# One Gelu for all MLP rows on ScalarE, with a changed start and end, in a fused attention and token-MLP kernel

## The chip, the cores and the metric

One core of a Trainium2 chip runs the kernel. The metric is the device time in microseconds of one execution. Before the change it is 704.06 us, the median of 3 runs (704.04 to 705.08).

## What is computed

The input x has 2048 rows of 512 columns. Two branches read its layer norm, and both are added to x.

```python
x = A_x
xn = _layernorm(x, axis=-1)
return x + _A_ref(xn, A_wqkv, A_wo) + _B_ref(xn, B_w1, B_b1, B_w2, B_b2)
# _A_ref: full softmax attention, H = 32 heads of Dh = 16 over S = 2048 rows
qkv = split(x @ wqkv);  scores = einsum("bhqd,bhkd->bhqk", q, k) * Dh ** -0.5
o = einsum("bhqk,bhkd->bhqd", softmax(scores), v);  return o @ wo
# _B_ref: an MLP over the rows (tokens), F = 1376
h = _layernorm(x);  u = gelu(einsum("bsd,sf->bdf", h, w1) + b1)   # tanh form of gelu
y = einsum("bdf,fs->bds", u, w2) + b2;  return y.transpose(0, 2, 1)
```

Inputs and output are bf16.

## The kernel before

**Attention.** Queries are cut into 4 query blocks of 512, heads into 8 groups of four. A pair of these is a block: 32 blocks in all (NBLK), and each has 16 key tiles of 128 keys. One key tile of one block is a score group, 512 of them (NGRP): four score products (line 558, K = 16 padded to 32 rows, four side by side in the array), each 128 keys by 512 queries. Its exponentials are taken in one of two ways:

- On ScalarE: two ACTIVATE Exp of 128 x 1024, each over two PSUM banks (line 566, tile pT). One PV pass of four products follows (line 578).
- On VectorE: four first passes that add a bias to the scores and write them as int16, which read as bf16 is an approximate power of two (line 612), and then two more planes shifted by a constant (line 617; NPL = 3 planes). Three PV passes follow. The planes lie in buffers of 128 x 2048 that are named after the memory they borrow: plx, which is their own, and x_sb, xn_sb, h_sb, w1blk and others once those are done with.

The PV result of a block lies in bank 6 and is copied by VectorE (line 1073). The denominators are inverted and spread out by small DMAs on SP's queue and POOL multiplies (line 1110, tiles oT and otmp).

**The dispatcher.** The order of every engine's instructions is fixed when the kernel is built. A dispatcher plays the program forward with its own planned costs (`occ`, `lat`) and at each step gives an engine the next thing that is ready. TensorE's rules are in `pe_step` and `pe_fill`: refill ScalarE's two bank pairs (banks 0 to 3) with scores as soon as they are free, give VectorE scores in banks 4, 5 and 7 when it has room, and otherwise issue PV passes and products of the side work. `d_pick1` decides which group VectorE may take: in the current block as long as D_KEEP groups remain open, at most D_AHEAD of the next, and in the last block only if it would be done before ScalarE (constant D_LAST). Side work is a list of chains (K, V and Q projections, the MLP), each with a due time in units of blocks. `two=True` marks VectorE instructions that the dispatcher keeps apart from long POOL instructions; planes are among them, first passes are not.

**The MLP.** After the second layer norm there are eleven chains `chain_ut`, one for each tile of 128 of the 1376 hidden rows (the last has 96): 16 products into one bank, a VectorE copy to u_sb with half of the bias (line 869), two VectorE products (lines 873 and 876), a ScalarE Tanh (line 879), and a VectorE product into gT (line 884). When all eleven are done (`ut_done`), sixteen chains `chain_yo` multiply gT with w2, one for each 128 output rows, in the order of `yt_order`. For the first three query blocks they add the attention's output product and x and store. For the last query block they put MLP + x into `part` (line 972), and the tail adds the attention.

**Start.** x comes in eight DMAs on SP's queue (four single tiles first), the first K and Q weights on ScalarE's queue. LN statistics of four tiles (NPRE), transposes, and the first K and Q tiles are written out by hand before the dispatcher starts.

**End.** Three output products and half of a fourth are done for each of the last four row tiles in banks 0 to 3 once ScalarE has no group left. `tail_epilogue` then takes the last block through VectorE in two halves of 256 columns (transpose, reciprocal, product, transpose: lines 1695 to 1703), ends the product (line 913), adds `part` on VectorE four times (line 1711) and stores on SP's queue.

Of the kernel before, what the change touches and what calls it, by code (L numbers as in the profile page):

```python
# [257 lines left out]
def bass_parallel_sum__softmax_full_mha__mixer_token_mlp__prompt_kernel(  # L258
# [18 lines left out]
    with ExitStack() as es:  # L277
# [32 lines left out]
        plx = sb("plx", [128, 2048], BF16)  # L310
# [10 lines left out]
        u_sb = sb("u_sb", [128, 512], F32)  # L321
        ga_sb = sb("ga_sb", [128, 512], F32)
# [36 lines left out]
        NPRE = 4  # L359

# [12 lines left out]
        def v_consts(i, eng):  # L373
# [5 lines left out]
            if i == 0:  # L379
                sc.add("dve", lambda e: e.memset(main[:, :, 16:17], 1.0), writes=[("Vone",)], occ=620)  # L380
# [12 lines left out]
        def ld_x(a, b_, lat):  # L393
            dma("sp", x_sb[:, a:b_, :],
                x2[128 * a:128 * b_, :].rearrange("(t p) d -> p t d", p=128),
                reads=[], writes=[("x", t) for t in range(a, b_)], name="ld_x", lat=lat)

        def ld_w(j, T0_, T1_, lat, q="act"):
# [4 lines left out]

        sc.add("act", lambda e: e.activation(r2[:, 0:1], zw[:, 0:1], ACTF.Identity), reads=[("zw",)], writes=[("r2",)],
               occ=1700)
# [22 lines left out]
        def late_consts():  # L428
# [10 lines left out]
            sc.add("dve", lambda e: e.tensor_scalar(b1h[:], b1c_bf[:], 0.5, None, ALU.mult), reads=[("b1c",), ("b1c2",)],  # L439
# [158 lines left out]
        plane_add(plx[:, :], [], "own")  # L598
# [99 lines left out]
        k_mm(1, 3, 0)  # L698
        qt0_mm(2, QB)
        ln_stats(NPRE)  # L700
        qt0_mm(3, 4)
        qt_evac(0, QB, "act", 0, 384)
        qt_evac(0, 4, "act", 384, 512, "QTh")
        k_mm(2, 3, 1)
        k_mm(3, 3, 2)
        qt_evac(1, 4, "act", 384, 512, "QTh")
        qt_evac(1, QB, "act", 0, 384)
        k_evac(1, 3, 3, 0)
# [25 lines left out]
        ut_done = [0]  # L734
        yo_done = {qb: 0 for qb in range(NQB)}
# [115 lines left out]
        def chain_ut(ft, due, rel):  # L851
# [15 lines left out]
            def u_evac():  # L867
                xb = bk[0]
                return sc.add("dve", lambda e: e.tensor_scalar(
                    u_sb[0:m, :], bank(xb)[0:m, :], 0.5, b1h[0:m, ft:ft + 1], ALU.mult, ALU.add),  # L870
                    reads=[("bank", xb), ("b1h",)], writes=[("u",)], occ=650, lat=800)
            steps.append(Step("dve", u_evac, 650, gate=lambda: ut_done[0] == ft, frees=True))
            steps.append(Step("dve", lambda: sc.add("dve", lambda e: e.scalar_tensor_tensor(
                ga_sb[0:m, :], u_sb[0:m, :], 4.0 * GELU_A, u_sb[0:m, :], ALU.mult, ALU.mult),
                reads=[("u",)], writes=[("ga",)], two=True, **T_DVE(512)), 610, two=True))
            steps.append(Step("dve", lambda: sc.add("dve", lambda e: e.scalar_tensor_tensor(
                ga_sb[0:m, :], ga_sb[0:m, :], 1.0, u_sb[0:m, :], ALU.add, ALU.mult),
                reads=[("ga",), ("u",)], writes=[("ga",)], two=True, **T_DVE(512)), 610, two=True))
            steps.append(Step("act", lambda: sc.add("act", lambda e: e.activation(  # L879
                ga_sb[0:m, :], ga_sb[0:m, :], ACTF.Tanh, scale=2.0 * GELU_C),  # L880
                reads=[("ga",)], writes=[("ga",)], occ=500, lat=680), 500))

            def fin():
                op = sc.add("dve", lambda e: e.scalar_tensor_tensor(
# [361 lines left out]
        def d_pick1():  # L1246
            skip()
            if ga[0] >= NGRP:
                return None
# [555 lines left out]
```

## Time and profile before

| | |
|---|---|
| median of 3 runs | 704.06 us (704.04 to 705.08) |
| the profiled execution | 704.31 us, its span 702.5 us |
| granted TensorE clock | 1.000 |
| exponentials on ScalarE (line 566) | 734 |
| first exponential starts | 11.45 us |
| MLP hidden tiles, copies of line 869 | 144.9 to 313.4 us |
| HBM read, written | 26.08 MB, 2.61 MB |

A busy share is the time in which an engine had at least one instruction in it. Instructions of one engine overlap at their ends, so a mean duration is longer than the distance between two starts. Matmul ends are modelled. "Idle before" names what ended the wait. Rows of a timeline begin with the start and the time taken in us.

### The profile page before, as it was taken

To read this page: it belongs to the slowest core of one execution; us is meant where nothing else is said; L and a number is where in the kernel's file an instruction comes from. 1 tells how busy PE (TensorE), PEld (TensorE's weight loads), DVE (VectorE), ACT (ScalarE), POOL (GpSimd) and SP (SyncE) were. 2 spreads that over 40 slices of the span, in tenths; PEclk is the share of its full clock that TensorE was granted. 3 is DMA by queue.
4 is the path that set the end of the run, shared out by engine and by line. 5 is a ranking of instruction groups with operands and counts; after the bars stand their busy time and mean duration, and the time that the engine had idled before them with its cause. 6 is when DMAs were issued, how large, how long until landed. Compare 5 with 4: busy or idle time off the path is not lost.

```text
span 702.5 us, 15631 instructions
## 1 busy us (share of the span) xinstructions
PE 670.9 (95%) x6238; PEld 200.8 (29%) x6238; DVE 665.5 (95%) x1155; ACT 684.5 (97%) x754; POOL 61.0 (9%) x89
## 2 busy tenths in 40 slices
PE   8999999999999999999999999999999999999987
PEld 4533333222222222222222222222222222222222
DVE  7889999999999999999999999999999999999998
ACT  6999999999999999999999999999999999999994
POOL 4510100000000000000000000000000000000000
PEclk9999999999999999999999999999999999999999
DMA  7024110022312132002221212111221022101001
GB/s 210 1 61 88 36 26 18 13 50 54 74 32 50 43 72 46 17 14 61 60 55 50 61 41 51 53 43 46 50 52 36 23 52 53 27 28 34 2 29 46
DMA packets 78368, 32.66 MB, mean 46 GB/s; under 512 B 63004, under 2 KB 74204, under 8 KB 78296
## 3 DMA queue, kind: packets, MB, share of 16 engines
q1 hardware_dynamic: 77240, 31.40, 18.2%
q8 instruction: 49, 0.80, 0.5%
q10 hardware_dynamic: 1056, 0.26, 0.2%
q14 instruction: 23, 0.19, 0.1%
HBM read 26.08 MB, written 2.61 MB: 41 GB/s over the span
## 4 chain that ended last, share of the span: by engine, by line
ACT 82%; PE 12%; DVE 4%; issue 1%; DMA 0%; DVEq 0%; SPq 0%
ACT pT L566 81%; PE ps L578 4%; PE ps L558 4%; DVE x_sb L612 2%; PE ps L895 2%; PE ps L905 1%; ACT ga_sb L879 1%; DVE plx L612 1%; PE ps L499 1%; DMA x_sb<-in_A_x_dram 0%; DVE x_sb L617 0%; DVE OT L1073 0%; PE ps L631 0%; PE ps L671 0%; DVE plx L617 0%
## 5 line engine op out<-in xcount | busy, mean ns | idle before, releaser
L566 ACT ACTIVATE pT<-ps 128x1024 bf16<-128x1024 f32 x734 | 676.5, 1125 | 2.1 <-PE ps L558 1.9
L558 PE MATMUL ps<-QT,KT 32*128 32x512 bf16 x2048 | 290.4, 384 | 21.2 <-ACT pT L566 16.7
L612 DVE TENSOR_SCALAR x_sb<-ps 128x512 int16<-128x512 f32 x404 | 274.2, 683 | 15.6 <-PE ps L558 2.5
L558 PEld LDWEIGHTS ps<-QT,KT 32*128 32x128 bf16 x2048 | 74.1, 91 | 278.5 <-ACT pT L566 266.1
L578 PE MATMUL ps<-pT,V 128*32 128x512 bf16 x1468 | 144.8, 390 | 2.1 <-DVE OT L1073 1.3
L612 DVE TENSOR_SCALAR plx<-ps 128x512 int16<-128x512 f32 x140 | 92.6, 680 | 1.9 <-PE ps L558 1.6
L617 DVE TENSOR_SCALAR x_sb<-x_sb 128x2048 int16<-128x2048 int16 x130 | 88.7, 684 | 1.9 <-PE ps L578 1.2
L578 PE MATMUL ps<-x_sb,V 128*32 128x512 bf16 x812 | 77.3, 382 | 0.0
L578 PEld LDWEIGHTS ps<-pT,V 128*32 128x32 bf16 x1468 | 37.2, 93 | 83.2 <-issue 73.4
L895 PE MATMUL ps<-gT,w2blk 128*128 128x512 bf16 (+1 forms) x176 | 57.1, 386 | 0.3 <-DVE h_sb L972 0.2
L858 PE MATMUL ps<-h_sb,w1blk 128*128 128x512 bf16 (+1 forms) x176 | 54.0, 386 | 0.3 <-DVE plx L612 0.2
L1110 POOL TENSOR_TENSOR oT<-OT,denb 128x512 bf16<-128x512 f32 x16 | 20.3, 1271 | 335.2 <-DVE x_sb L617 181.9
L617 DVE TENSOR_SCALAR x_sb<-plx 128x2048 int16<-128x2048 int16 x63 | 43.0, 686 | 2.1 <-PE ps L578 1.4
L1110 POOL TENSOR_TENSOR otmp<-OT,denb 128x512 bf16<-128x512 f32 x15 | 19.1, 1273 | 272.5 <-DVE x_sb L617 173.3
L499 PE MATMUL ps<-xnT,wqkv_sb 128*128 128x512 bf16 (+1 forms) x188 | 40.6, 315 | 1.6 <-DVE xnT L495 0.7
L578 PE MATMUL ps<-x_sb,V17b 128*32 128x512 bf16 x420 | 41.2, 382 | 0.2 <-DVE x_sb L617 0.2
L617 DVE TENSOR_SCALAR plx<-x_sb 128x2048 int16<-128x2048 int16 x46 | 31.5, 685 | 1.5 <-PE ps L578 1.5
L578 PE MATMUL ps<-plx,V 128*32 128x512 bf16 x264 | 26.0, 381 | 0.2 <-DVE plx L617 0.2
L612 DVE TENSOR_SCALAR xn_sb<-ps 128x512 int16<-128x512 f32 x36 | 24.6, 683 | 1.6
L578 PEld LDWEIGHTS ps<-x_sb,V 128*32 128x32 bf16 x812 | 21.3, 96 | 16.0 <-issue 10.2
L1073 DVE COPY OT<-ps 128x512 f32<-128x512 f32 x31 | 21.0, 677 | 0.0
L499 PE MATMUL ps<-wqkv_sb,xnT 128*128 128x128 bf16 x256 | 20.8, 220 | 0.0
(84 smaller groups left out, 355.3 us busy)
## 6 DMA issues: line engine op xcount, KB each, us to landing
denb<-rec_scr SPq DMA_DIRECT2D x124, 64.0 KB, 2.1
w1blk<-in_B_w_dram SPq DMA_DIRECT2D x10, 512.0 KB
w2blk<-in_B_w_dram SPq DMA_DIRECT2D x16, 320.0 KB, 3.4
xres<-in_A_x_dram SPq DMA_DIRECT2D x16, 128.0 KB, 2.2
QT<-qst SPq DMA_DIRECT2D x120, 16.0 KB, 1.8
out_dram<-osb SPq DMA_DIRECT2D x14, 128.0 KB, 1.7
wqkv_sb<-in_A_wqkv_dram SPq DMA_DIRECT2D x3, 384.0 KB, 8.1
x_sb<-in_A_x_dram SPq DMA_DIRECT2D x2, 512.0 KB, 6.5
```

Of the source, the lines that this page charges most:

```text
L499: return sc.add("pe", lambda e: e.matmul(dst, lhsT=lhsT, rhs=rhs, start=(ct == 0), stop=(ct == NCT - 1)), reads=reads, writes=[("bank", bk ...
L558: return sc.add("pe", lambda e: e.matmul(bank(bk), lhsT=KT[32 * r:32 * r + 32, T, 128 * kt:128 * (kt + 1)], rhs=QT[32 * r:32 * r + 32, slo ...
L566: return sc.add("act", lambda e: e.activation(pT[:, buf, :], ps[:, slot * 1024:(slot + 1) * 1024], ACTF.Exp, scale=EXP_SCALE), reads=[("ba ...
L578: return sc.add("pe", lambda e: e.matmul(bank(PV_BANK)[32 * r:32 * r + 32, :], lhsT=vt_[:, off:off + 32], rhs=rhs, start=start, stop=stop, ...
L612: return sc.add("dve", lambda e: e.tensor_scalar(plane_i[pb][:, 512 * r:512 * (r + 1)], bank(bk), BIAS, 0.0, ALU.add, ALU.max), reads=[("b ...
L617: return sc.add("dve", lambda e: e.tensor_scalar(plane_i[pb], plane_i[pb0], float(SHIFT[j]), BITS_MAX, ALU.add, ALU.min), reads=[("pl", pb ...
L858: op = sc.add("pe", lambda e: e.matmul(bank(xb)[0:m, :], lhsT=w1blk[:, slot, st, 0:m], rhs=h_sb[:, st, :], start=(st == 0), stop=(st == NT ...
L879: steps.append(Step("act", lambda: sc.add("act", lambda e: e.activation(ga_sb[0:m, :], ga_sb[0:m, :], ACTF.Tanh, scale=2.0 * GELU_C), read ...
L895: op = sc.add("pe", lambda e: e.matmul(bank(xb), lhsT=w2blk[0:m, slot, ft, :], rhs=gT[0:m, ft, :], start=first, stop=last), reads=([("w2bl ...
L905: return sc.add("pe", lambda e: e.matmul(bank(bk), lhsT=oT[:, par, T, 128 * sti:128 * (sti + 1)], rhs=wo_c[:, T, :], start=first, stop=las ...
L1073: op = sc.add("dve", lambda e: e.tensor_copy(OT32[:, eb, :], bank(PV_BANK)), reads=[("bank", PV_BANK)], writes=[("OT32", eb)], **T_DVE(512))
L1110: op = sc.add("pool", lambda e: e.tensor_tensor(dst, OT32[:, eb, :], denb[:, :], ALU.mult), reads=[("OT32", eb)] + [("denb", r) for r in r ...
```

## The change

1. **Gelu.** `chain_ut` keeps one VectorE instruction, which adds the bias and writes bf16 into gT. When all eleven tiles are there, a chain "gelu" issues two ScalarE ACTIVATE Gelu_apprx_tanh in place: one over 128 x 10 x 512, one over 96 x 512. The dispatcher plans a table load (TABLE = 1283) with each. `chain_yo` waits for their planned end. u_sb and ga_sb are gone, plx holds two planes.
2. **Start.** The four single tiles of x alternate between SP's and ScalarE's queue; the first K weights move to SP's queue behind them. The ones column of V is written by ScalarE in place of a VectorE memset. In the order written out by hand, statistics, evacuations and filler products move.
3. **End.** The last rows' chains for row tiles 14 and 15 move to the end of `yt_order` and take in two of the output products. Of tiles 12 and 13 `part` is split by POOL into a bf16 value and a bf16 rest, which TensorE adds into the bank by the identity; ScalarE then copies the bank out. Tiles 14 and 15 are still added by VectorE. The tail's banks are 4, 5, 7 and 0, and the last block goes through VectorE in one piece of 512 columns.
4. **Dispatcher.** VectorE may be given scores whatever its backlog if ScalarE's next bank pair is more than FAR = 1300 away; D_LAST goes from 5500 to 7500, TOL from 140 to 150.

```diff
-        plx = sb("plx", [128, 2048], BF16)
+        plx = sb("plx", [128, 2 * 2048], BF16)
...
-        u_sb = sb("u_sb", [128, 512], F32)
-        ga_sb = sb("ga_sb", [128, 512], F32)
...
+        TABLE = 1283.0
...
-            if i == 0:
-                sc.add("dve", lambda e: e.memset(main[:, :, 16:17], 1.0), writes=[("Vone",)], occ=620)
...
-        for t in range(NPRE):
-            ld_x(t, t + 1, 2150 + 60 * t)
-        ld_w(1, 0, 1, 2900)
-        ld_w(0, 0, 1, 3000)
+        for t in range(NPRE):
+            ld_x(t, t + 1, 2150 + 200 * (t // 2), "sp" if t % 2 == 0 else "act")
+        ld_w(1, 0, 1, 3000, "sp")
+        ld_w(0, 0, 1, 3100)
...
+        sc.add("act", lambda e: e.activation(v17_views[0][1][:, :, 16], KT[:, 1, 0:NKT * H], ACTF.Identity, bias=1.0),
+               reads=[("KTt", 1, t) for t in range(4)], writes=[("Vone",)], occ=490, lat=670)
...
         ln_stats(0)
         ln_stats(1)
+        ln_stats(2)
         ln_norm(0)
         transpose_mm(0, 4, 0)
         xnT_evac(0, 1, 4, 0, "act")
-        zeros(6)
-        ln_stats(2)
+        zeros(3, 330)
         ln_stats(3)
-        k_mm(0, KB, 0)
-        qt0_mm(0, QB)
-        zeros(1)
         ln_norm(1)
         transpose_mm(1, 5, 0)
         ln_norm(2)
         xnT_evac(1, 1, 5, 0, "act")
-        k_evac(0, 1, KB, 0)
+        k_mm(0, KB, 0)
         transpose_mm(2, 0, 0)
         ln_norm(3)
-        xnT_evac(2, 1, 0, 0, "act")
+        xnT_evac(2, 1, 0, 0, "dve")
+        qt0_mm(0, QB)
         transpose_mm(3, 1, 0)
         xnT_evac(3, 1, 1, 0, "dve")
+        k_evac(0, 1, KB, 0, "act")
...
             def u_evac():
                 xb = bk[0]
-                return sc.add("dve", lambda e: e.tensor_scalar(
-                    u_sb[0:m, :], bank(xb)[0:m, :], 0.5, b1h[0:m, ft:ft + 1], ALU.mult, ALU.add),
-                    reads=[("bank", xb), ("b1h",)], writes=[("u",)], occ=650, lat=800)
...
+                op = sc.add("dve", lambda e: e.tensor_scalar(
+                    gT[0:m, ft, :], bank(xb)[0:m, :], b1h[0:m, ft:ft + 1], None, ALU.add),
+                    reads=[("bank", xb), ("b1h",)], writes=[("gT", ft)], occ=650, lat=800)
                 ut_done[0] += 1
                 return op
-            steps.append(Step("dve", fin, 610, two=True))
+            steps.append(Step("dve", u_evac, 650, gate=lambda: ut_done[0] == ft, frees=True))
...
+        def gelus():
+            for m, f0, f1, occ in ((128, 0, NFT - 1, TABLE + 64.0 + (NFT - 1) * 512 / 1.2),
+                                   (MLAST, NFT - 1, NFT, TABLE + 64.0 + 512 / 1.2)):
+                op = sc.add("act", lambda e, m=m, f0=f0, f1=f1: e.activation(
+                    gT[0:m, f0:f1, :], gT[0:m, f0:f1, :], ACTF.Gelu_apprx_tanh),
+                    reads=[("gT", f) for f in range(f0, f1)], writes=[("gT", f) for f in range(f0, f1)], occ=occ)
+            ge_done[0] = op.end
+            return op
...
-        yt_order = [4 * qb + i for qb in (0, 1, 3, 2) for i in range(4)]
+        HL = (0, 1)
+        PT = (0, 0, 2, 2)
+        TBANK = (4, 5, EX_BANK, 0)
...
+                return sc.add("pool", lambda e: e.tensor_copy(hilo[:, i, 0, :], part[:, c, :]), reads=[("part", c)],
+                              writes=wk, occ=1266, lat=1330)
+            hl_done[0] += 1
+            return sc.add("pool", lambda e: e.tensor_tensor(hilo[:, i, 1, :], part[:, c, :], hilo[:, i, 0, :], ALU.subtract),
+                          reads=[("part", c), ("hilo", i, 0)], writes=wk[:1], occ=1266, lat=1330)
...
+        yt_order = list(range(8)) + [12, 13] + list(range(8, 12)) + [14, 15]
...
                 def gate():
-                    return len(oT_done[qb]) == NG and ut_done[0] == NFT
+                    return len(oT_done[qb]) == NG and ge_done[0] <= now[0]
...
+        bg.append(Chain("gelu", [Step("act", gelus, gate=lambda: ut_done[0] == NFT)], 0.0, 0.0))
...
-        D_LAST = 5500.0
+        D_LAST = 7500.0
...
-        TOL = 140.0
+        TOL = 150.0
...
-            if dve_backlog(t) < D_HUNGRY and t + 226 + (SWITCH if sc.cfg != "S" else 0) <= lim:
+            far = t_s is not None and 1e9 > t_s > t + FAR
+            if (dve_backlog(t) < D_HUNGRY or far) and t + 226 + (SWITCH if sc.cfg != "S" else 0) <= lim:
...
-            half(0)
-            half(1)
-            for c in range(4):
-                fin(c)
+            for c in range(4):
+                op_half(1, 1, c, TBANK[c], False, True)
+            for c in range(4):
                 st = 12 + c
+                bk = TBANK[c]
                 buf, key = (osb, ("osb", c)) if c < 2 else (xres, ("xres", c - 2))
+                if c in HL:
+                    evac("act", buf[:, c % 2, :], bank(bk), reads=[("bank", bk)], writes=[key])
+                else:
+                    sc.add("dve", lambda e, c=c, bk=bk, buf=buf: e.tensor_tensor(buf[:, c % 2, :], bank(bk), part[:, c, :],
+                                                                                 ALU.add),
+                           reads=[("bank", bk), ("part", c)], writes=[key], **T_DVE(512))
```

More of the change, by code (lines that the diff above doesn't have):

```diff
@@ L596, in plane_add @@
             plane_home.append(home)
-        plane_add(plx[:, :], [], "own")
+        for j in range(2):
+            plane_add(plx[:, 2048 * j:2048 * (j + 1)], [], "own")
         for reg, nm in ((x_flat, "x"), (xn_flat, "xn")):
@@ L876, in chain_ut @@
[L876 to L881, printed above, removed]
@@ L979, in gate @@
                 def gate():
-                    return ut_done[0] == NFT
+                    return ge_done[0] <= now[0] and all(G in oT_done[qb] for G in range(2 * PT[sti]))
             steps.append(Step("dve", fin, 610, frees=True))
@@ L1247, in d_pick1 @@
             skip()
-            if ga[0] >= NGRP:
+            if ga[0] >= NGRP or tail["over"]:
                 return None
@@ L1708, in fin @@
-            def fin(c):
+            NB = 512 // 32
+            rc = den_s[:, 0, 0:NB]
+            dn = denb[:, :].rearrange("p (c m) -> p c m", m=32)
+            wt = gT[:, 0, :].rearrange("p (c m) -> p c m", m=32)
+            dk, wk = ("denb", 0), ("gT", 0)
+            sc.add("dve", lambda e: e.transpose(denb[:, :], bank(PV_BANK)),
+                   reads=[("bank", PV_BANK)], writes=[("denb", r) for r in range(4)], **T_DVE(512))
+            sc.add("dve", lambda e: e.reciprocal(rc, dn[:, :, 16]), reads=[dk], writes=[("den_s", 0)], occ=190, lat=320)
```

107 lines of the change are left out of this document (57 added, 50 removed).

## The prediction

> **What bounds the kernel now.** I read the page's busy line, its chain and its costliest groups first, to find the engine whose work sets the end.
>
> ```profile
> span 702.5 us, 15631 instructions
> PE 670.9 (95%) x6238; PEld 200.8 (29%) x6238; DVE 665.5 (95%) x1155; ACT 684.5 (97%) x754; POOL 61.0 (9%) x89
> ACT 82%; PE 12%; DVE 4%; issue 1%; DMA 0%; DVEq 0%; SPq 0%
> L566 ACT ACTIVATE pT<-ps 128x1024 bf16<-128x1024 f32 x734 | 676.5, 1125 | 2.1 <-PE ps L558 1.9
> L612 DVE TENSOR_SCALAR x_sb<-ps 128x512 int16<-128x512 f32 x404 | 274.2, 683 | 15.6 <-PE ps L558 2.5
> L612 DVE TENSOR_SCALAR plx<-ps 128x512 int16<-128x512 f32 x140 | 92.6, 680 | 1.9 <-PE ps L558 1.6
> L612 DVE TENSOR_SCALAR xn_sb<-ps 128x512 int16<-128x512 f32 x36 | 24.6, 683 | 1.6
> ```
>
> The chain lies on ScalarE for 82% of the span: 734 exponentials that waited 2.1 us in all. But ScalarE does not own this work. There are 512 score groups; a group is either two exponentials on ScalarE or six VectorE instructions (four first passes of line 612 and two planes of line 617). Line 612 ran 404 + 140 + 36 = 580 times, so 145 groups went to VectorE; the other 367 are the 734 exponentials. The dispatcher hands a group to whichever engine is free, so VectorE time that comes free shortens ScalarE's list. TensorE looks as busy, so I asked the waits and the windows.
>
> ```profile
> PEld ps L558 <- ACT pT L566: 266.1, 665, 0.8
> 145.00:318.00 173.00, 168.72 (x1507) 46.56 (x1504) 169.26 (x282) 173.00 (x195) 10.17 (x8) 1.00 0.20 46
> ```
>
> TensorE's weight loads for scores waited 665 times for an exponential to free its banks, so TensorE follows ScalarE. The window 145 to 318 us is the stage of the eleven MLP tiles (columns: PE, PEld, DVE, ACT, POOL): VectorE is busy 169.26 of 173 us, ScalarE throughout. A freed VectorE slot there meets a queue of work.
>
> Durations overlap, so I price by the distance between starts, from two timelines.
>
> ```profile
> 301.90 0.75 ACT L879 ACTIVATE ga_sb<-ga_sb 128x512 f32<-128x512 f32 x1
> 302.42 13.98 ACT L566 ACTIVATE pT<-ps 128x1024 bf16<-128x1024 f32 x15
> 316.13 0.62 ACT L879 ACTIVATE ga_sb<-ga_sb 96x512 f32<-96x512 f32 x1
> 316.66 28.63 ACT L566 ACTIVATE pT<-ps 128x1024 bf16<-128x1024 f32 x31
> 300.45 0.68 DVE L876 SCALAR_TENSOR_TENSOR ga_sb<-ga_sb,u_sb 128x512 f32<-128x512 f32 x1
> 301.05 0.68 DVE L617 TENSOR_SCALAR x_sb<-plx 128x2048 int16<-128x2048 int16 x1
> 313.43 0.74 DVE L869 TENSOR_SCALAR u_sb<-ps,b1h 96x512 f32<-96x512 f32 x1
> 314.08 0.24 DVE L1088 RECIPROCAL den_s<-den_s 128x16 f32<-128x16 f32 x1
> ```
>
> Fifteen exponentials from 302.42 to 316.13 are 0.914 us each; a tanh holds ScalarE 0.52 us (301.90 to 302.42). A VectorE instruction of this size holds it 0.60 us (300.45 to 301.05), the copy of line 869 0.65 us (313.43 to 314.08). One group thus costs ScalarE 1.83 us, or VectorE 3.60 us.
>
> **VectorE's side of the MLP.** Per tile the change drops lines 873, 876 and 884 and keeps one copy.
>
> ```profile
> L873 DVE SCALAR_TENSOR_TENSOR ga_sb<-u_sb x11: 643/679/777, 146.2 to 314.2; 128x512 f32<-128x512 f32 x10, 96x512 f32<-96x512 f32 x1
> L876 DVE SCALAR_TENSOR_TENSOR ga_sb<-ga_sb,u_sb x11: 625/678/684, 147.4 to 315.4; 128x512 f32<-128x512 f32 x10, 96x512 f32<-96x512 f32 x1
> L884 DVE SCALAR_TENSOR_TENSOR gT<-ga_sb,u_sb x11: 678/681/692, 150.0 to 317.2; 128x512 bf16<-128x512 f32 x10, 96x512 bf16<-96x512 f32 x1
> L869 DVE TENSOR_SCALAR u_sb<-ps,b1h x11: 736/740/751, 144.9 to 313.4; 128x512 f32<-128x512 f32 x10, 96x512 f32<-96x512 f32 x1
> ```
>
> 33 x 0.60 = 19.8 us go. The copy does one operation for two and writes bf16; no row has that form, so 0.60 to 0.65 us, 0 to 0.55 us saved over eleven, I take 0.3. Freed: 20.1 us.
>
> **ScalarE's side.** Eleven tanh go, 11 x 0.52 = 5.7 us. Two Gelu instructions (5120 columns, then 512) and the switches of the function table come.
>
> ```profile
> L404 ACT ACT_TABLE_LOAD x1 | 1.3, 1283 | 0.7 <-PEq L1790 0.7
> L519 ACT ACTIVATE QT<-ps,qmask 128x384 bf16<-128x384 f32 x2 | 1.2, 584 | 0.5 <-PE ps L499 0.5
> L519 ACT ACTIVATE QT<-ps,qmask 128x128 bf16<-128x128 f32 x2 | 0.6, 362 | 0.0
> ```
>
> The one table load serves Identity, Exp and Tanh here; Gelu isn't shown. I assume that it needs its own table: one load before, one back, 2.57 us. Price per column: exponential against tanh (0.914 - 0.52)/512 = 0.77 ns; the two Q copies (584 - 362)/256 = 0.867 ns. So 5120 columns are 0.52 + 4608 x 0.77 = 4.07 to 4.51 us, I take 4.3 (nearer the exponential in size); the second is 0.52. An exponential lasts 1.125 us but holds ScalarE 0.914, so emptying the pipe before each load adds about 0.21, twice. Gelu also waits for the last copy, 0 to 0.65 us, I take 0.3. Sum 4.3 + 0.52 + 2.57 + 0.42 + 0.3 = 8.1 us, bounds 7.2 to 8.8; net of the tanh +2.4 (1.5 to 3.1).
>
> Queued behind that block on ScalarE are the exponentials; their scores fill both bank pairs and TensorE has only VectorE's groups, PV and filler. The new rule FAR lets TensorE feed VectorE then, so VectorE works on; without that cover 8.1 us of VectorE are lost, which the exchange below prices at 8.1 x 0.34 = 2.7 us.
>
> [...]
>
> **Sharing it out.** Let n groups move to VectorE. ScalarE changes by 2.4 - 1.83n, VectorE by -20.1 + 3.60n; both end together at n = 22.5/5.43 = 4.1, which is 2.4 - 7.6 = **-5.2 us** (-5.8 to -4.7 over the bounds). By the same exchange one us of VectorE is worth 1.83/5.43 = 0.34 us of the end, one us of ScalarE 3.60/5.43 = 0.66. TensorE pays two more PV passes a group (three planes for one), small beside its waits above.
>
> **Other edits in the middle.** The MLP's second product waits for the block.
>
> ```profile
> 371.99 0.36 SPq L352 DMA_DIRECT2D out_dram<-osb  x1
> 405.55 1.27 POOL L1110 TENSOR_TENSOR oT<-OT,denb 128x512 bf16<-128x512 f32 x1 [20.37 <-DVE x_sb L617]
> ```
>
> Its chains start some 5 us later (8.1, less the three products and tanh that followed the last copy). Who waits: the fourth store of the first 512 rows is at 371.99, and the multiply of block 16 that needs it (line 1110) at 405.55, so 33 us cover it. The hi/lo split adds four POOL instructions, 4 x 1.27 us, on an engine 9% busy; planes may not run beside them, but first passes may: nothing, or 5 us of VectorE x 0.34 = 1.7 us without first passes to do. The second own plane buffer and the wider TOL I take at nothing, -1 to +1.
>
> **Start.**
>
> ```profile
> 1.19 2.98 DMA x_sb<-in_A_x_dram
> 4.20 0.69 DVE L444 BATCH_NORM_STATS2 stats<-x_sb 128x6 f32<-128x512 bf16 x1 [0.26 <-DMA x_sb<-in_A_x_dram]
> 11.45 7.45 ACT L566 ACTIVATE pT<-ps 128x1024 bf16<-128x1024 f32 x8
> 19.41 2.85 ACT L566 ACTIVATE pT<-ps 128x1024 bf16<-128x1024 f32 x3 [0.51 <-PE ps L558]
> ```
>
> The second tile of x holds up VectorE for 0.26 us; with ScalarE's queue it lands earlier, and the small K copy leaves VectorE while one evacuation comes to it. The K weights go behind two x tiles on SP, hidden as long as they land before the first K products. The first exponential may come 0.5 us sooner, but at 19.41 ScalarE waits again for later tiles, which depend on VectorE. I take -0.3 (-0.6 to +0.2).
>
> **End.**
>
> ```profile
> 688.58 4.95 ACT L566 ACTIVATE pT<-ps 128x1024 bf16<-128x1024 f32 x5
> 694.46 0.39 PE L578 MATMUL ps<-x_sb,V17b 128*32 128x512 bf16 x4
> 694.90 0.45 DVE L1695 STREAM_TRANSPOSE denb<-ps 128x256 f32<-128x256 f32 x1 [0.65 <-PE ps L578]
> 695.95 0.45 DVE L1703 STREAM_TRANSPOSE otmp<-gT 128x256 bf16<-128x256 bf16 x1
> 697.33 0.45 DVE L1703 STREAM_TRANSPOSE otmp<-gT 128x256 bf16<-128x256 bf16 x1
> 697.80 1.29 DVE L1711 TENSOR_TENSOR osb<-ps,h_sb 128x512 bf16<-128x512 f32 x2
> 699.00 1.28 DVE L1711 TENSOR_TENSOR xres<-ps,h_sb 128x512 bf16<-128x512 f32 x2
> 698.52 0.95 SPq L352 DMA_DIRECT2D out_dram<-osb  x2
> 699.71 0.93 SPq L352 DMA_DIRECT2D out_dram<-xres  x2
> ```
>
> Two half chains run from 694.90 to 697.78, 2.88 us; one half is 1.50, of it 0.90 transposes. One full chain: transposes between 0.68 (a 512-column pass) and 0.90 each, I take 0.72, and 0.60 to 0.75 between: 2.2 us, 0.65 saved. Four sums in series end at 700.28; two on VectorE beside two copies on ScalarE end near 699.3. Then the stores bind: four of about 0.45 us on SP's queue from 698.35 end at 700.1, for 700.64 now. I take -0.6 (-0.9 to 0). D_LAST stops VectorE 2.0 us sooner in the last block: 2.0 x 0.34 = +0.7, less up to 0.4 since the last PV, a plane at 694.46, need not trail the last exponential (ended 693.53). Net +0.3 (-0.4 to +0.9).
>
> **Sum:** -5.2 - 0.3 - 0.6 + 0.3 = -5.8 us. The profiled execution took 704.31 us (span 702.5 and 1.8 around it), 0.25 above the median 704.06; -5.8 gives 698.5 against it, 698.3 against the median.
>
> **The rivals.**
> - *A longer switch.* If ScalarE must let a whole exponential run out before each load, 1.125 for 0.21 us twice, its net is +4.2; n = 24.3/5.43 = 4.5, -4.0 - 0.6 = 699.5. No row shows a switch. [...] Chance 0.13.
> - *Gelu shares the exponential's table,* so no switch comes, the change of table being only the plan's: net 2.4 - 2.57 - 0.42 = -0.6, n = 3.6, -7.2 - 0.6 = 696.3. The load of this trace already covers three functions; a fourth is unlikely. 0.05.
> - *More than the freed time is used.* VectorE stood idle 702.5 - 665.5 = 37 us. If FAR, TOL and the second plane fill a quarter, 9 x 0.34 = 3 us more: 695. 0.13.
> - *Half of it is used,* since VectorE's new groups wait for banks: n = 2, 2.4 - 3.7 - 0.6 = 702.2. 0.11.
> - *Slower: no group moves.* TensorE's fixed order lies behind ScalarE's 8.1 us block and its plane or bank limits keep VectorE at 145 groups; then ScalarE only gains the +2.4, with the ends 706. It decides below one group moved (1.83n < 2.4 - 0.6). For it: TensorE at 95%. Against: the 665 waits and a VectorE that is full where the work goes. 0.08.
>
> **How the numbers follow.** The forecast has 0.50, with its own range 696.5 to 700. What a measurement here can tell is about 0.2%, 1.4 us. Faster holds the forecast, the first three rivals and most of the fourth, 0.88; within 0.2% 0.04; slower 0.08. The range 693.5 to 702.0 leaves out the slower rival, the worse part of the half case, and the far end of the better case.
>
> **What would show it.** Right: about 726 exponentials (734 - 8), some 149 groups (596 passes of line 612's successor), two more table loads of 1.28 us, one Gelu of 4.1 to 4.6 us, ScalarE's gap between exponentials there near 8 us while VectorE stays busy, the last exponential to the last store about 0.6 us shorter. Wrong: exponentials still at 734, a VectorE hole beside the Gelu, or a gap of 10 us.

## The result, and the profile after

| | before | after | the same kernel again |
|---|---|---|---|
| median (six runs each) | 704.47 us | 700.39 us (699.05 to 701.9) | 699.37 us (698.58 to 702.28) |
| ratio to before, 95% interval | 1 | 0.9938 [0.9927, 0.995] | 0.9935 [0.9922, 0.9948] |
| profiled execution, its span | 704.31, 702.5 us | 701.9, 700.1 us | 699.21, 697.4 us |
| exponentials on ScalarE | 734 | 726 | 726 |
| last exponential's end to the span's end | 8.97 us | 8.46 us | 8.46 us |

Faster by 0.6%: 4.1 us where 5.8 were forecast, inside the range. Every later group of runs was made beside runs of before of its own (medians 704.31 to 704.55), and its ratio is to those. From the page of the kernel after: its span, busy line, chain, and the group of the exponentials (count, busy, mean ns, idle before and what ended it).

```profile
span 700.1 us, 15532 instructions
PE 657.4 (94%) x6195; PEld 198.4 (28%) x6277; DVE 657.8 (94%) x1139; ACT 683.0 (98%) x742; POOL 64.3 (9%) x93
ACT 84%; PE 9%; DVE 4%; issue 1%; POOL 0%; DMA 0%; DVEq 0%
L565 ACT ACTIVATE pT<-ps 128x1024 bf16<-128x1024 f32 x726 | 667.8, 1136 | 5.2 <-PE ps L557 4.9
```

The chain is ScalarE's still. Eight exponentials are gone, and ScalarE waits for scores 5.2 us where it waited 2.1: 3.1 us of the gain went there. The groups by form on VectorE:

```profile
L612 DVE TENSOR_SCALAR x_sb<-ps 128x512 int16<-128x512 f32 x268 | 183.3, 686 | 12.0 <-PE ps L557 3.3
L612 DVE TENSOR_SCALAR plx<-ps 128x512 int16<-128x512 f32 x272 | 178.5, 682 | 3.6 <-PE ps L557 3.2
L612 DVE TENSOR_SCALAR xn_sb<-ps 128x512 int16<-128x512 f32 x48 | 32.9, 686 | 2.7 <-PE ps L557 0.8
```

With 4 on h_sb and 4 on w1blk these are 596 first passes, 149 groups: the 145 of before and four more. plx now takes 272 of them, where it took 140. ScalarE's timeline around the Gelu (start, us taken, count):

```profile
289.71 19.44 ACT L565 ACTIVATE pT<-ps 128x1024 bf16<-128x1024 f32 x21
309.16 1.28 ACT L880 ACT_TABLE_LOAD   x1
310.46 4.99 ACT L880 ACTIVATE gT<-gT 128x5120 bf16<-128x5120 bf16 x2
315.45 1.28 ACT L565 ACT_TABLE_LOAD   x1
316.75 5.61 ACT L565 ACTIVATE pT<-ps 128x1024 bf16<-128x1024 f32 x6
```

The two Gelu instructions by themselves (shortest, median and longest in ns, first and last start, forms):

```profile
L880 ACT ACTIVATE gT<-gT x2: 612/2541/4470, 310.5 to 314.8; 128x5120 bf16<-128x5120 bf16 x1, 96x512 bf16<-96x512 bf16 x1
```

Two loads, so Gelu does not share the exponential's table. The last exponential before ends at 309.15 and the load starts at 309.16. The block is 7.6 us, 309.16 to 316.75. The windows before, beside and behind it (columns: length, PE, PEld, DVE, ACT, POOL, granted clock, DMA share, GB/s) show whether VectorE went on:

```profile
300.00:309.16 9.16, 9.16 (x96) 2.59 (x95) 8.83 (x17) 9.14 (x10) 0.00 (x0) 1.00 0.07 16
309.16:316.73 7.57, 7.02 (x48) 2.06 (x46) 7.25 (x12) 7.55 (x4) 1.27 (x1) 1.00 0.16 47
316.73:326.00 9.27, 8.99 (x60) 2.44 (x59) 9.25 (x16) 9.26 (x12) 0.00 (x0) 1.00 0.23 55
```

7.25 of 7.57 us: no hole. The tail of the kernel after:

```profile
692.87 0.72 DVE L1734 STREAM_TRANSPOSE denb<-ps 128x512 f32<-128x512 f32 x1 [0.66 <-PE ps L577]
694.37 0.71 DVE L1741 STREAM_TRANSPOSE otmp<-gT 128x512 bf16<-128x512 bf16 x1
695.76 1.09 ACT L492 ACTIVATE osb<-ps 128x512 bf16<-128x512 f32 x2 [4.12 <-PE ps L907]
696.19 1.29 DVE L1752 TENSOR_TENSOR xres<-ps,h_sb 128x512 bf16<-128x512 f32 x2 [1.12 <-PE ps L907]
697.27 0.94 SPq L350 DMA_DIRECT2D out_dram<-xres  x2
```

One chain of 2.21 us (692.87 to 695.08) took the place of the two that lasted 2.88, with 0.72 us a transpose.

**A ledger for every kernel.** ScalarE's own list reads a span in four terms: start of the first exponential, N x 0.914 us, the MLP's block on ScalarE (11 tanh 5.7 us, the Gelu block 7.6), and the tail from the last exponential's end. What is left between the first and the last exponential I call stalls: ScalarE's waits and whatever stretched an exponential's distance. In one_table, where the loads are left out, the block is 4.9. The span, and so the terms of one row, are those of the profiled execution; the median is that of all runs:

| kernel | N | first exp. | stalls | tail | span | median | ratio [95%] |
|---|---|---|---|---|---|---|---|
| before | 734 | 11.45 | 5.3 | 8.97 | 702.5 | 704.47 | 1 |
| after | 726 | 11.04 | 9.3 | 8.46 | 700.1 | 700.39 | 0.9938 [0.9927, 0.995] |
| after_again | 726 | 11.15 | 6.5 | 8.46 | 697.4 | 699.37 | 0.9935 [0.9922, 0.9948] |
| gelu_only | 730 | 11.03 | 5.2 | 8.89 | 700.2 | 702.17 | 0.9976 [0.9966, 0.9986] |
| no_gelu | 734 | 11.02 | 5.5 | 8.38 | 701.7 | 703.68 | 0.9992 [0.9983, 1.0] |
| no_far | 728 | 12.75 | 5.0 | 9.07 | 700.0 | 700.76 | 0.9945 [0.9933, 0.9958] |
| one_table | 728 | 12.52 | 6.6 | 8.56 | 698.2 | 697.32 | 0.9909 [0.9895, 0.9923] |
| dummy_dve | 732 | 12.36 | 6.7 | 8.50 | 704.4 | 706.33 | 1.0026 [1.0017, 1.0035] |
| gelu_rules | 726 | 11.34 | 6.6 | 8.62 | 697.9 | 698.04 | 0.9911 [0.99, 0.9923] |
| defer400 | 722 | 10.90 | 9.7 | 10.14 | 698.5 | 701.76 | 0.9971 [0.9958, 0.9984] |
| old_start | 726 | 11.04 | 4.6 | 8.17 | 695.2 | 697.79 | 0.9903 [0.9889, 0.9917] |
| one_queue | 724 | 12.26 | 8.4 | 9.78 | 700.0 | 702.94 | 0.9973 [0.9961, 0.9984] |
| more_zeros | 726 | 10.92 | 10.1 | 10.61 | 703.0 | 703.94 | 0.9994 [0.9985, 1.0003] |
| one_plane | 730 | 10.97 | 9.7 | 7.86 | 703.6 | 703.62 | 0.9992 [0.9979, 1.0006] |

From before to after_again: list -8 x 0.914 = -7.3, block +1.9, first exponential -0.3, tail -0.5, stalls +1.2, together -5.0; the spans differ by 5.1.

### The profile page after: what moved, and what is told of

It reads as the page before. It is cut to its first block, busy times and chain, and to the rows that moved or that the text cites. A ratio compares the mean times of both kernels' runs of the same rounds, so it can differ in the third digit from the quotient of the medians.

```text
span 700.1 us, 15532 instructions
## 1 busy us (share of the span) xinstructions
PE 657.4 (94%) x6195; PEld 198.4 (28%) x6277; DVE 657.8 (94%) x1139; ACT 683.0 (98%) x742; POOL 64.3 (9%) x93
## 4 chain that ended last, share of the span: by engine, by line
ACT 84%; PE 9%; DVE 4%; issue 1%; POOL 0%; DMA 0%; DVEq 0%
ACT pT L565 83%; PE ps L557 3%; PE ps L577 3%; DVE x_sb L612 1%; PE ps L889 1%; ACT gT L880 1%; DVE plx L612 1%; PE ps L498 1%; DVE x_sb L617 1%; PE ps L899 1%; POOL r L480 0%; DMA x_sb<-in_A_x_dram 0%; DVE stats L443 0%; PE ps L631 0%; ACT QT L518 0%
## 5 line engine op out<-in xcount | busy, mean ns | idle before, releaser
L565 ACT ACTIVATE pT<-ps 128x1024 bf16<-128x1024 f32 x726 | 667.8, 1136 | 5.2 <-PE ps L557 4.9
L612 DVE TENSOR_SCALAR x_sb<-ps 128x512 int16<-128x512 f32 x268 | 183.3, 686 | 12.0 <-PE ps L557 3.3
L612 DVE TENSOR_SCALAR plx<-ps 128x512 int16<-128x512 f32 x272 | 178.5, 682 | 3.6 <-PE ps L557 3.2
L617 DVE TENSOR_SCALAR x_sb<-plx 128x2048 int16<-128x2048 int16 x90 | 61.3, 685 | 0.9 <-PE ps L577 0.6
L577 PE MATMUL ps<-plx,V 128*32 128x512 bf16 x556 | 54.0, 386 | 0.4
L577 PE MATMUL ps<-x_sb,V 128*32 128x512 bf16 x532 | 52.1, 388 | 1.7 <-DVE OT L1093 1.3
L617 DVE TENSOR_SCALAR plx<-x_sb 128x2048 int16<-128x2048 int16 x71 | 48.7, 687 | 2.5 <-PE ps L577 2.2
L617 DVE TENSOR_SCALAR x_sb<-x_sb 128x2048 int16<-128x2048 int16 x51 | 34.7, 686 | 1.4 <-PE ps L577 1.3
L612 DVE TENSOR_SCALAR xn_sb<-ps 128x512 int16<-128x512 f32 x48 | 32.9, 686 | 2.7 <-PE ps L557 0.8
L617 DVE TENSOR_SCALAR plx<-plx 128x2048 int16<-128x2048 int16 x32 | 21.9, 685 | 1.1 <-PE ps L577 0.8
```

The costliest lines, as they stand in the source:

```text
L565: return sc.add("act", lambda e: e.activation(pT[:, buf, :], ps[:, slot * 1024:(slot + 1) * 1024], ACTF.Exp, scale=EXP_SCALE), reads=[("ba ...
L577: return sc.add("pe", lambda e: e.matmul(bank(PV_BANK)[32 * r:32 * r + 32, :], lhsT=vt_[:, off:off + 32], rhs=rhs, start=start, stop=stop, ...
L612: return sc.add("dve", lambda e: e.tensor_scalar(plane_i[pb][:, 512 * r:512 * (r + 1)], bank(bk), BIAS, 0.0, ALU.add, ALU.max), reads=[("b ...
L617: return sc.add("dve", lambda e: e.tensor_scalar(plane_i[pb], plane_i[pb0], float(SHIFT[j]), BITS_MAX, ALU.add, ALU.min), reads=[("pl", pb ...
```

## The experiments

**The theory:** VectorE time freed in the MLP pays for four groups, at 0.34 us a microsecond, if VectorE is fed beside the block; start and end give less than 1 us. **The rivals:** the gain is not Gelu's but the rules' and the second plane's; the loads hide nothing or cost more than their length; the start or the end gives or takes more than I priced.

### The same kernel once more

> The changed kernel unaltered, to see its undisturbed trace. In the first profile of it the granted clock fell to 0.50 from about 470.5 to 477 us and ScalarE lost some 3.4 us there. If that dip is an accident of one execution, this profile has a span near 697.3 us and the six earlier times split into 699.1 without a dip and 700.4 to 701.9 with one. If the dip belongs to the fixed order, it comes at the same place again.

0.9935 [0.9922, 0.9948] beside 0.9938, with the same 726; its profiled span is 697.4 beside 700.1. What differs between the two executions is one place. After:

```profile
466.17 1.27 POOL L1130 TENSOR_TENSOR otmp<-OT,denb 128x512 bf16<-128x512 f32 x1 [20.73 <-DMA denb<-rec_scr]
466.43 1.55 DVE L617 TENSOR_SCALAR xn_sb<-plx 128x2048 int16<-128x2048 int16 x1
470.39 0.62 PE L577 MATMUL ps<-x_sb,V 128*32 128x512 bf16 x4 [1.03 <-DVE OT L1093]
471.59 1.02 ACT L565 ACTIVATE pT<-ps 128x1024 bf16<-128x1024 f32 x1 [1.45 <-PE ps L557]
473.10 1.02 ACT L565 ACTIVATE pT<-ps 128x1024 bf16<-128x1024 f32 x1 [0.49 <-PE ps L557]
474.61 1.02 ACT L565 ACTIVATE pT<-ps 128x1024 bf16<-128x1024 f32 x1 [0.49 <-PE ps L557]
476.55 215.09 ACT L565 ACTIVATE pT<-ps 128x1024 bf16<-128x1024 f32 x234 [0.92 <-PE ps L557]
```

and again:

```profile
466.29 1.27 POOL L1130 TENSOR_TENSOR otmp<-OT,denb 128x512 bf16<-128x512 f32 x1 [20.80 <-DMA denb<-rec_scr]
466.48 1.63 DVE L617 TENSOR_SCALAR xn_sb<-plx 128x2048 int16<-128x2048 int16 x1
470.50 0.40 PE L577 MATMUL ps<-x_sb,V 128*32 128x512 bf16 x4 [1.03 <-DVE OT L1093]
471.27 217.68 ACT L565 ACTIVATE pT<-ps 128x1024 bf16<-128x1024 f32 x237 [1.08 <-PE ps L557]
```

In both, a POOL multiply starts beside a plane of line 617, which takes 1.55 or 1.63 us instead of 0.69. VectorE then copies the PV result late, TensorE waits 1.03 us for it, and ScalarE 1.45 or 1.08 for TensorE. In after, four PV products then take 0.62 instead of 0.40, and the windows show the clock granted there:

```profile
470.00:473.50 3.50, 3.11 (x26) 0.60 (x26) 2.59 (x5) 1.56 (x3) 0.00 (x0) 0.52 0.06 11
473.50:477.00 3.50, 3.50 (x34) 0.64 (x26) 2.03 (x4) 2.09 (x3) 0.00 (x0) 0.50 0.00 0
```

The granted clock was 0.5 for some 7 us (1.00 in after_again), and ScalarE waited 3.35 us instead of 1.08. That accounts for 2.3 of the 2.8 us of stalls between the two executions. It doesn't explain all of the spread, as the expectation had it: only the slowest run of each six has a granted clock under 1 (701.9 us at 0.994, 702.28 at 0.995), and the other five of each, at 1.000, still lie some 1.5 us apart.

### Gelu alone

Before, with only these parts of the diff:

```diff
-            steps.append(Step("dve", fin, 610, two=True))
+            steps.append(Step("dve", u_evac, 650, gate=lambda: ut_done[0] == ft, frees=True))
...
+        bg.append(Chain("gelu", [Step("act", gelus, gate=lambda: ut_done[0] == NFT)], 0.0, 0.0))
```

and `gelus` and the gates on ge_done that go with them. plx keeps one plane; start, end and rules are those of before.

> The kernel before with the Gelu part alone (one copy per tile, two Gelu instructions, the wait of the second product for them); start, end, FAR, TOL, D_LAST and the plane buffers as before. Its fixed order holds 730 exponentials on ScalarE, 4 fewer than before and 4 more than the whole change. Theory A, the end follows ScalarE's list: 4 x 0.914 = 3.7 us less, 7.6 - 5.7 = 1.9 us more for the table block, so 1.8 us faster than before, ratio 0.997. Theory B, the prediction's step, that freed VectorE time is shared out in full whatever the dispatcher's rules: 5.2 us faster, ratio 0.993.

702.17, 0.9976 [0.9966, 0.9986]: less than half of the gain. 730 exponentials: two groups moved, not four. VectorE beside the block (311.3 to 319 here), as windows and as a timeline row:

```profile
311.30:319.00 7.70, 7.46 (x54) 3.12 (x48) 3.29 (x6) 7.65 (x5) 1.27 (x1) 1.00 0.12 32
```

```profile
320.45 0.69 DVE L611 TENSOR_SCALAR x_sb<-ps 128x512 int16<-128x512 f32 x1 [5.75 <-PE ps L557]
```

VectorE was busy 3.29 of 7.70 us and lost 5.75 in one piece, waiting for scores from TensorE. This is the hole that the prediction feared, in the kernel without FAR.

### Everything but Gelu

After, with the old `chain_ut` and no chain "gelu"; u_sb and ga_sb are back, and plx has one plane:

```diff
-        plx = sb("plx", [128, 2 * 2048], BF16)
+        plx = sb("plx", [128, 2048], BF16)
...
+        u_sb = sb("u_sb", [128, 512], F32)
+        ga_sb = sb("ga_sb", [128, 512], F32)
```

> The whole change without the Gelu part: old VectorE products and tanh per tile, one plane buffer of its own as before (no room for two), but the new start, end, FAR, TOL and D_LAST. 734 exponentials as before. From the two traces: first exponential 0.41 us sooner (11.04 for 11.45), last exponential to the end of the span 8.46 for 8.97 us, so 0.9 us faster, ratio 0.9987. Rival, the ends carry most of the gain: 3 us or more faster, ratio 0.996 or less. Rival, D_LAST eats what the ends gain: 1.000.

703.68, 0.9992 [0.9983, 1.0]: start, end, FAR, TOL and D_LAST without Gelu and the second plane are worth nothing that this measurement tells from no change; the 0.9987 of the expectation lies inside the interval too. N stays 734.

### Gelu with the rules and the second plane, old start and old end

```diff
-        plx = sb("plx", [128, 2048], BF16)
+        plx = sb("plx", [128, 2 * 2048], BF16)
...
-        D_LAST = 5500.0
+        D_LAST = 7500.0
...
-        TOL = 140.0
+        TOL = 150.0
...
-            if dve_backlog(t) < D_HUNGRY and t + 226 + (SWITCH if sc.cfg != "S" else 0) <= lim:
+            far = t_s is not None and 1e9 > t_s > t + FAR
+            if (dve_backlog(t) < D_HUNGRY or far) and t + 226 + (SWITCH if sc.cfg != "S" else 0) <= lim:
```

(against gelu_only)

> The kernel before with the Gelu part and the four settings of the dispatcher (FAR, TOL 150, D_LAST 7500, second own plane buffer), but the old start and the old end. 726 exponentials. If the Gelu and these settings together make the gain, it is the changed kernel less the new ends: 0.5 to 0.9 us slower than it, about 700.1, ratio to before 0.994. If the new ends and the Gelu need each other: near the Gelu alone, 702.2.

698.04, 0.9911 [0.99, 0.9923]: 4.1 us under gelu_only (0.65% by the ratios), with two more groups moved, and faster than the whole change, though its interval touches that of after_again. So here the middle makes more than all of the gain, and the new start and end together take about 0.24% back. In no_gelu they did not: what they are worth hangs on the rest of the order. The tail is 8.62 with the old end, 8.89 in gelu_only, so it lost 0.27 us without the new end. Of the four settings D_LAST is the one that acts there, but it was not tried alone.

### FAR off

```diff
-        FAR = 1300.0
+        FAR = 1e8
```

> The changed kernel with FAR out of reach, so TensorE may not feed VectorE during the table block unless its backlog is empty. 728 exponentials for 726. Theory A, by the list: 2 x 0.914 = 1.8 us slower than the changed kernel, about 701 without a dip. Prediction's figure for a lost cover: 2.7 us slower, with a VectorE hole of about 8 us beside the Gelu. Rival, the rule does nothing since VectorE's banks are full anyway: no difference and no hole.

700.76 against 699.37: +1.4 us, but the ratios' intervals overlap (0.9945 [0.9933, 0.9958]), so the loss itself isn't resolved. N is 728, one group less, and the hole is back:

```profile
320.01 1.49 DVE L612 TENSOR_SCALAR x_sb<-ps 128x512 int16<-128x512 f32 x2 [4.92 <-PE ps L557]
```

4.92 us x 0.34 = 1.7 us fits; the prediction's 2.7 took the whole block for lost.

### One own plane

```diff
-        plx = sb("plx", [128, 2 * 2048], BF16)
+        plx = sb("plx", [128, 2048], BF16)
...
-        for j in range(2):
-            plane_add(plx[:, 2048 * j:2048 * (j + 1)], [], "own")
+        plane_add(plx[:, :], [], "own")
```

> The changed kernel with one plane buffer of VectorE's own instead of two. 730 exponentials for 726. By ScalarE's list: 4 x 0.914 = 3.7 us slower than the changed kernel, 703.0. By the prediction, which took the second buffer at nothing, -1 to +1: 699.4 to 700.4.

703.62, 0.9992 [0.9979, 1.0006]: +4.2 us, the whole gain. N 730: two groups back, 2 x 2 x 0.914 = 3.7 us. So two of the four groups hang on the second buffer. Its 4 KB in a partition (2048 bf16) are as much as Gelu freed: u_sb and ga_sb, 2 KB each (512 f32). Of this kernel's 9.7 us of profiled stalls 2.1 (waits of 0.74, 0.92 and 0.48 for scores, from 690.15 us on) lie in the last of the 40 slices of its page, the only one whose granted clock is below 0.9 (0.8 to 0.9).

### VectorE's products put back

```diff
+            for _ in range(3):
+                steps.append(Step("dve", lambda: sc.add("dve", lambda e: e.scalar_tensor_tensor(
+                    osb_f[0:m, :, :], xres_f[0:m, :, :], 1.0, xres_f[0:m, :, :], ALU.add, ALU.mult),
...
```

Gelu stays; three products whose result nobody reads are added to each of the eleven tiles.

> The changed kernel with VectorE's freed time filled again: after each tile's copy three VectorE products of the old form (f32, 128 x 512) on unused buffers, so 33 instructions of 0.60 us come back and nothing else changes. The order holds 732 exponentials for 726. By ScalarE's list: 6 x 0.914 = 5.5 us slower than the changed kernel, about 704.9, as slow as before. By the prediction's exchange: 19.8 x 0.34 = 6.7 us slower, 706. Rival, VectorE has 40 us of idle time that takes them up: no difference, 699.4.

706.33, 1.0026 [1.0017, 1.0035]: +7.0 us over after_again for 33 x 0.60 = 19.8 us of VectorE, 0.35 us a microsecond; the exchange said 0.34, 6.7 us. Three groups went back (N 732). The closeness is in part luck: in the profiled spans, 704.4 and 697.4, the list makes 5.5 of the 7.0, which is 0.28 a microsecond, and a later first exponential makes 1.2 (12.36 for 11.15), more than 100 us before the first of these products.

### No change of table

```diff
-        TABLE = 1283.0
+        TABLE = 0.0
...
-                    gT[0:m, f0:f1, :], gT[0:m, f0:f1, :], ACTF.Gelu_apprx_tanh),
+                    gT[0:m, f0:f1, :], gT[0:m, f0:f1, :], ACTF.Tanh),
```

Tanh of the same rows, so the function computed is another one.

> The changed kernel with Tanh in place of Gelu in the two big ScalarE instructions, and no load planned for them (what it computes in the MLP is then tanh of u, not gelu). Tanh shares the exponential's table, so the two loads go: 2 x 1.28 us. The order holds 728 exponentials for 726. By ScalarE's list: -2.57 + 2 x 0.914 = -0.7 us against the changed kernel, so 698.7. [...] Rival, the block is hidden beside VectorE's work: no difference, or slower by the two exponentials, 701.

697.32, 0.9909 [0.9895, 0.9923]: 2.05 us under after_again. ScalarE's timeline has the two ACTIVATEs without loads:

```profile
310.40 4.98 ACT L880 ACTIVATE gT<-gT 128x5120 bf16<-128x5120 bf16 x2
315.28 7.62 ACT L565 ACTIVATE pT<-ps 128x1024 bf16<-128x1024 f32 x8
```

The last exponential before the block, here and then in after:

```profile
309.48 1.16 ACT L565 ACTIVATE pT<-ps 128x1024 bf16<-128x1024 f32 x1
307.99 1.16 ACT L565 ACTIVATE pT<-ps 128x1024 bf16<-128x1024 f32 x1
```

From its start to the start of the first exponential behind the block, ScalarE took 5.80 us here (309.48 to 315.28) and 8.76 in after (307.99 to 316.75). Two switches thus cost 2.96 us: 2.57 of loads and 0.39 of instructions that ran to their end instead of overlapping with the next. So the loads alone are not the whole cost: one switch took 1.48, 0.2 more than its load. N rose to 728: with 2.96 us of ScalarE free, the exchange gives 0.5 of a group back to it (2.96/5.43), and it was one. The list then has -2.96 + 1.83 = -1.1 us; the other 0.9 of the 2.05 isn't settled.

### The old start

After, with the start of before: the ones column by memset, the old written order, and

```diff
-            ld_x(t, t + 1, 2150 + 200 * (t // 2), "sp" if t % 2 == 0 else "act")
-        ld_w(1, 0, 1, 3000, "sp")
-        ld_w(0, 0, 1, 3100)
...
+            ld_x(t, t + 1, 2150 + 60 * t)
+        ld_w(1, 0, 1, 2900)
+        ld_w(0, 0, 1, 3000)
```

> The changed kernel with the old start (x on SP's queue alone, K and Q weights on ScalarE's, old order written out by hand, the ones column by VectorE); Gelu, rules and end as changed. 726 exponentials as there. If the new start is what costs (its first x tile was read at 3.5 to 4.0 us for 3.07, TensorE stood still 1.1 to 2.0 us, and in three of seven profiles its first products ran at half rate and the first exponential came at 12.4 to 12.8 for 11.0 to 11.5): first exponential 11.0 to 11.5, 0.4 to 1.3 us faster than the changed kernel, 698.3. By the prediction, that the new start brings 0.3 us: 699.7 to 700.4.

697.79, 0.9903 [0.9889, 0.9917], below after's intervals: 1.6 us under after_again by the medians and 2.3 by the ratios. It has **the lowest median of the kernels that compute the same function**, though its interval overlaps with that of gelu_rules. With this end and these rules the new start costs; it doesn't give 0.3. VectorE's first statistics and first normalization and TensorE's first transposes, old_start:

```profile
3.08 0.65 DVE L443 BATCH_NORM_STATS2 stats<-x_sb 128x6 f32<-128x512 bf16 x1
4.94 0.41 DVE L463 TENSOR_SCALAR xn_sb<-x_sb,mv 128x512 bf16<-128x512 bf16 x1
5.41 0.40 PE L631 MATMUL ps<-ident,xn_sb 128*128 128x128 bf16 x4 [0.68 <-DVE xn_sb L463]
11.04 7.46 ACT L565 ACTIVATE pT<-ps 128x1024 bf16<-128x1024 f32 x8
```

no_far, which has the new start:

```profile
3.96 0.70 DVE L443 BATCH_NORM_STATS2 stats<-x_sb 128x6 f32<-128x512 bf16 x1 [2.74 <-DMA x_sb<-in_A_x_dram]
6.38 0.38 DVE L463 TENSOR_SCALAR xn_sb<-x_sb,mv 128x512 bf16<-128x512 bf16 x1
6.82 0.40 PE L631 MATMUL ps<-ident,xn_sb 128*128 128x128 bf16 x4 [1.97 <-DVE xn_sb L463]
8.55 0.63 PE L498 MATMUL ps<-xnT,wqkv_sb 128*128 128x128 bf16 x4
12.75 7.46 ACT L565 ACTIVATE pT<-ps 128x1024 bf16<-128x1024 f32 x8
```

With the new start the first statistics began later (3.96, 3.73 in after_again, 3.61 in after, against 3.08), and the first normalization later still (6.38, 6.15 and 6.03 against 4.94), since the new written order puts the statistics of a third tile ahead of it. TensorE stood 1.1 to 2.0 us before its first transposes. In three profiles of this start (no_far, one_table, dummy_dve) four products then took 0.61 to 0.63 us instead of 0.39, and the first exponential came at 12.4 to 12.8 instead of 10.9 to 11.2. The window of no_far in which its slow products begin has a granted clock of 0.50:

```profile
8.00:9.00 1.00, 0.85 (x9) 0.86 (x10) 0.83 (x3) 0.21 (x1) 0.49 (x1) 0.50 1.09 346
```

It stays at 0.50 until 11.00, with 0.84 in the microsecond before and 0.95 in the one behind, which is about 3.4 us at half the clock. In one_table and dummy_dve, whose products are as slow, every microsecond up to 13.00 shows 1.00. That the hole brought the slow products about isn't shown: after took 0.40 for its first transposes behind a hole of 1.18 us, and before 0.61 behind one of 0.18, both at a granted clock of 1.00.

That the new start loses in this kernel is thus shown; where it loses isn't. after_again and old_start differ by 0.1 in the first exponential and by 1.8 in stalls, and 1.1 of those are the overlap at 466 us, which another start's order happens not to have.

### Two tries to mend the start

```diff
-            ld_x(t, t + 1, 2150 + 200 * (t // 2), "sp" if t % 2 == 0 else "act")
-        ld_w(1, 0, 1, 3000, "sp")
+            ld_x(t, t + 1, 2150 + 200 * (t // 2), "sp")
+        ld_w(1, 0, 1, 2900)
```

> The changed kernel with the four single x tiles on SP's queue alone and both first weights on ScalarE's queue, as before; the rest of the new start stays. 724 exponentials for 726. If the two queues side by side hold up the first tile: its statistics start at 3.1 instead of 3.5 to 4.0, TensorE's hole shrinks by as much, first exponential near 10.6, and with two exponentials fewer 697.0. If the queue makes no difference: statistics at 3.5 or later, 697.6 to 698.6 from the list alone.

```diff
-        zeros(9, 430)
+        zeros(13, 430)
```

> The changed kernel with 13 filler products at the start instead of 9, to close TensorE's hole between 5.3 and 6.6 us. 726 exponentials. The first x tile still read at 3.5 to 4.0. If the hole is what leaves TensorE at half rate in some executions: transposes at 0.39 or 0.40 us each group, first exponential at 11.0 to 11.2, the times within half a us of each other near 699. If not: half rate products or 12.4 in some, and the same spread as the changed kernel.

Both were slower: 702.94 and 703.94. With x on one queue the first statistics did start earlier, but TensorE's hole did not shrink, and the first exponential came at 12.26 where near 10.6 was expected:

```profile
3.24 0.69 DVE L443 BATCH_NORM_STATS2 stats<-x_sb 128x6 f32<-128x512 bf16 x1 [2.01 <-DMA x_sb<-in_A_x_dram]
6.79 0.61 PE L631 MATMUL ps<-ident,xn_sb 128*128 128x128 bf16 x4 [1.51 <-DVE xn_sb L463]
```

So the two queues are not what makes the hole: the three statistics ahead of the first normalization are still there. With four more filler products TensorE had no hole, took 0.39 to 0.43 us for four transposes at a granted clock of 1.00, and brought the first exponential to 10.92, as wanted. But each edit also changes the order of all that follows, and that decided the times:

```profile
374.84 317.56 ACT L565 ACTIVATE pT<-ps 128x1024 bf16<-128x1024 f32 x346 [3.34 <-PE ps L557]
```

in more_zeros, a like wait of 2.47 us at 352.15 in one_queue, and tails of 10.61 in more_zeros and 9.78 in one_queue. So neither says what the start itself is worth in time.

### Fewer exponentials still

```diff
-        DEFER = 250.0
+        DEFER = 400.0
```

> The changed kernel with DEFER at 400 instead of 250: TensorE may hold scores for ScalarE back longer if a VectorE bank is about to come free. 722 exponentials for 726. If the end follows ScalarE's list and nothing else: 4 x 0.914 = 3.7 us faster than the changed kernel, 695.7. If the held back scores leave ScalarE waiting: its stalls grow by as much or more, 699 or slower.

N fell to 722, two groups more than after, and the time rose to 701.76. Stalls of 9.7 us (2.27 at 373.53, 1.18 at 349.15) and a tail of 10.14 ate 3.7 us of list. The count of exponentials alone doesn't forecast the time.

## Why the prediction was right, and where not

- **Right: the exchange and the count.** 734 - 8 = 726 and 596 passes, as forecast; 19.8 us of VectorE put back cost 5.5 us of list and 7.0 in all (6.7 by the exchange). ScalarE's list fell by 7.3 - 1.9 = 5.4 us, forecast 5.2.
- **Right: the block.** Forecast 8.1 us; counted as the prediction counts, from where the next exponential could have started, it was 8.76 - 0.91 = 7.8. The first Gelu took 4.47, near the upper bound. Emptying the pipe, put at 0.42, was 0.39 (one_table). The 0.3 for the last copy did not come: it ended at 308.4, before the load at 309.16. *A longer switch* falls: it put a whole exponential, 1.125 us, on top of each load; here a switch was 1.48, the load's 1.28 and 0.2 of lost overlap. *A shared table* falls too: there are two loads.
- **Right by luck: four groups.** The step *Sharing it out* gave all four to Gelu's freed time, and took second plane and TOL "at nothing, -1 to +1". Gelu alone moved two groups (702.17), close to the rival *half of it is used* with its 702.2. Taken out of the whole change, the second plane is worth 4.2 us, the whole gain, and FAR some 1.4 (put at 2.7), which isn't resolved. TOL and D_LAST were not tried alone. The forecast counted freed time on VectorE, and not the buffers that a group must hold from its first pass to its last PV: that VectorE then stood for want of a place, not of time, is my reading of the two groups that one_plane lost, not a row of its trace.
- **Wrong: the start.** Put at -0.3 (-0.6 to +0.2); undoing it gained 1.6 us, though only 0.1 of that lies in the first exponential of the profiled executions. The prediction looked at the wait of 0.26 us for the second tile alone. That wait went, but the step left out what the same edit does to the first tile (statistics 0.4 to 0.9 us later) and to the first normalization, which now stands behind three statistics; it had no term for TensorE's hole (1.1 to 2.0 us) and the products after it (0.61 to 0.63 us for four in three profiles, instead of 0.39). The first exponential at 11.04 in after, for 11.45 before, only looks like the forecast gain: with the old start it came at 11.03 to 11.45 in four profiles, with the new one at 10.90 to 12.75 in eight (one_queue and more_zeros, which change it, left out), 0.4 us later on average.
- **Right in size, not resolved in time: the end.** The tail fell by 0.5 us from before to after. Of gelu_rules and old_start, which differ in the end alone, the tails are 8.62 and 8.17: of the 0.67 us by which the new last chain is shorter (2.21 us, as worked out), 0.45 stayed. The medians, 698.04 and 697.79, are not told apart. D_LAST was put at a loss of 0.3; no run has it alone.
- **Smaller:** the copy of line 869 became no cheaper (0.66 between starts, no saving of 0.3).
- **Missing: the stalls.** They grew by 1.2 us in one execution and 4.0 in the other, from one overlap and one dip of the clock to 0.5 for some 7 us. The medians' distance to the forecast, 1.1 and 2.1 us, is of that size. old_start, which has neither, shows a span of 695.2.

Not tried: after without the one overlap at 466 us alone, since every edit of the plan moves all that follows. That the overlap starts the wait is read from two profiles, not shown by a kernel that differs in nothing else.

## What to carry to other kernels

Price freed time by what the receiving engine needs to use it: place, operands and the order in front of it; a buffer may be worth more than the instructions that were removed. In a kernel whose order is fixed when it is built, split the list (count times distance) from the stalls, and judge an edit by both, since an edit in one place moves waits in all others. Try the parts alone: here the version with the lowest median leaves one of them out.

## What the hardware showed that was not expected

- A plane of line 617 that started behind a POOL multiply of 1.27 us took 1.55 and 1.63 us instead of 0.69 (after and after_again), and ended 0.54 and 0.55 us behind the multiply. The other way round the multiply paid: in old_start a plane started at 252.68 and took its 0.69, and the multiply that started 0.05 us behind it took 1.76 (the row below). In these three pairs the one that started second took longer than elsewhere; why, no run here shows.

```profile
252.73 1.76 POOL L1131 TENSOR_TENSOR otmp<-OT,denb 128x512 bf16<-128x512 f32 x1 [20.18 <-DVE plx L612]
```

- The same wait of TensorE (1.03 us at 470 us) was followed by 7 us at a clock of 0.5 in one execution and by 1.00 in the other. It is one part of the spread between executions of one kernel; some 1.5 us of it came at a clock of 1.000.
- The ones column of V, 512 single bf16 values written apart from each other, took ScalarE 2.36 us, where a dense 128 x 512 copy took 0.60. It lay in the start, beside the wait for x.
